# Reordering the first chunk of a fused attention, gated-product and MoE kernel

## The chip, the cores and the metric

The kernel runs on one core of one Trainium2 chip. The metric is the device time of one execution in microseconds (us). The engines are named as in the profile: PE is TensorE, with PEld its weight loads; DVE is VectorE, ACT ScalarE, POOL GpSimd, and SP is SyncE, which issues most of the DMA transfers.

## The reference

Three stages follow one another. First comes attention with a sliding window of 128 positions and a linear bias per head, for 4 batches of 8 heads, 576 positions and 64 columns:

```
rel = pos[:, None] - pos[None, :]
mask = (rel >= 0) & (rel < 128)
scores = where(mask, q @ k.T / 8 + bias, -1e9)
x = softmax(scores) @ v            # then laid out as [2304, 512]
```

Then a gated product, `x = ((x @ w_a) * (x @ w_b)) @ w_out`, with an inner width of 1536. Last, a mixture of eight experts with top-1 choice:

```
logits = x @ w_gate + modality_bias[modality_id]
e = argmax(logits);  gate_w = softmax(logits)[e]
out = gate_w * (relu(x @ w1[e]) @ w2[e])     # e per token, F = 1024
```

The weights of the gated product arrive as 64-bit floats.

## The kernel before

The 2304 tokens are cut into 7 chunks of 3, 2, 2, 3, 3, 3 and 2 tiles of 128 (`CH`). An item is one pair of heads on one tile of one chunk: scores on PE, masking and maximum on DVE, the exponential on ACT, the reciprocal on DVE, the normalisation on ACT, PE transposes (`pt_tr`), copies into `pc` (half ACT, half DVE), masks by POOL into `pt`, and the product with v on PE. Chunk 0 has 12 items (`n0`). They run first, as a software pipeline of attention alone; items `n0` and `n0 + 1`, the first two of chunk 1, are scored in it too.

From then on the gated product of chunk c goes in 12 steps of 128 inner columns (`NJ`): `step0` for chunk 0, `step` for chunks 1 to 5, `step6` for the last. Each step holds, beside its own matmuls, some items of the attention of the next chunk. A step j of PE is: `psa` (12 matmuls into the bank ab0), `psb` (12 into ab1), the attention's matmuls, and `mm_out` of the step before (`pend`). DVE forms `gf = psb * asb`, where ACT copied `asb` from `psa`. psb of the next step may start only when gf has read its bank. Numbers in the 32-bit format of the matmuls are split in a high and a low half, and three of the four products are kept; in chunk 0 `mm_out` multiplies the unsplit 32-bit weight and gf instead (L506).

In chunk 0 the 64-bit weights are also converted: `wab_jobs(j)` gives five jobs for w_a and w_b of step j, `one` and twice `more` on DVE (together `f64_ops`), `hi` on ACT and `rest` on DVE. `wo_jobs(j)` gives three on DVE for w_out. The raw and the converted w_out tiles share four rotating buffers (`WOB`). DVE's row in `step0` mixes these jobs with the items' reciprocals, `rest` first.

A tile of x that leaves the gated product is routed: its eight logits, the largest and its index, the gate, and the rank of each token within its expert. The logits come either from PE (four transposes, L522, and eight matmuls with the gate weights, L530), or, for chunks listed in `RD`, from DVE: eight dots of a 128x512 tile with a broadcast gate weight (`rd_dot`, L592, one expert per step, each tile of the chunk). These dots stand in step j = 1 to 8 of the next chunk. The rest (`route_fin`) is one short row of DVE instructions (stage a, L537 to L556), a gate (L549, L550), and a rank, for which PE multiplies by a triangle (`tri`) and adds `ones` times `osum`; DVE then adds the tile's one-hot to `osum` (L567), so that ranks follow one another.

The order on PE, DVE and ACT is the order in which the program is written from chunk 0's steps on. SP's and POOL's are made by a scheduler.

Of the kernel before, what the change touches and what calls it, by code (L numbers as in the profile page):

```python
# [21 lines left out]
def attn_moe_moe2(ctx: ExitStack, tc, q, k, v, moe_w_a, moe_w_b, moe_w_out, modality_id,  # L22
# [185 lines left out]
    def a_prep_q(a):  # L208
        n = a.nt * P
        if a.c not in S32:  # L210
            for h in range(2):
# [556 lines left out]
    with tc.manual_schedule():  # L768
# [74 lines left out]
        st_s(n0 + 1)
        i1 = live[n0 + 1]
        score_red(i1)
        score_inv(i0)
        score_nrm(i0)
        pt_tr(i0)
        score_exp(i1)
        pt_cp(i0)  # L850
# [621 lines left out]
```

## Time and profile before

| | |
|---|---|
| runs (us) | 829.16, 830.38, 830.48 |
| median (us) | 830.38 |
| profiled execution (us) | 828.85 |
| its span (us) | 827.1 |
| mean granted clock of TensorE | 0.993 |
| busy: PE, DVE, ACT, POOL | 97%, 66%, 56%, 28% |
| DMA | 145 MB, 175 GB/s on average |

Of the 40 equal slices of the span, PE is busy for 90% or more in 37. The others are the second (80%), the third (70%; 41 to 62 us, the change from the pipeline to chunk 0's steps) and the last. A row of a timeline is an instruction or a run of equal ones; its duration includes what overlaps with the next, so the distance of two starts is the better measure of what one costs. The square bracket names what ended the engine's idle time.

### The profile page before, as it was taken

To read this page: it belongs to the slowest core of one execution; us is meant where nothing else is said; L and a number is where in the kernel's file an instruction comes from. 1 tells how busy PE (TensorE), PEld (TensorE's weight loads), DVE (VectorE), ACT (ScalarE), POOL (GpSimd) and SP (SyncE) were. 2 spreads that over 40 slices of the span, in tenths; PEclk is the share of its full clock that TensorE was granted. 3 is DMA by queue.
4 is the path that set the end of the run, shared out by engine and by line. 5 is a ranking of instruction groups with operands and counts; after the bars stand their busy time and mean duration, and the time that the engine had idled before them with its cause. 6 is when DMAs were issued, how large, how long until landed. Compare 5 with 4: busy or idle time off the path is not lost.

```text
span 827.1 us, 14384 instructions
## 1 busy us (share of the span) xinstructions
PE 798.5 (97%) x4686; PEld 722.1 (87%) x4686; DVE 547.4 (66%) x1571; ACT 461.3 (56%) x1161; POOL 235.3 (28%) x365
## 2 busy tenths in 40 slices
PE   9879999999999999999999999999999999999994
PEld 7767877999899999999999999998888998989893
DVE  7789997777676776767876776378476444447420
ACT  6854446877688866666667643223436444547410
POOL 5353231533333333333333332020233030115101
PEclk9999999999999999999999999999999999999998
DMA  8994346677666875555556444467428554549201
GB/s 241 369 381 138 121 130 204 198 222 229 183 163 176 206 191 163 146 159 133 161 159 152 127 128 123 140 225 218 145 90 300 186 186 127 180 128 323 107 16 41
DMA packets 78629, 145.13 MB, mean 175 GB/s; under 512 B 14095, under 2 KB 41903, under 8 KB 78544
## 3 DMA queue, kind: packets, MB, share of 16 engines
q1 hardware_dynamic: 74992, 134.39, 53.5%
q0 software_dynamic: 3552, 9.73, 3.2%
q8 instruction: 39, 0.64, 0.3%
q14 instruction: 46, 0.38, 0.1%
HBM read 118.16 MB, written 22.12 MB: 170 GB/s over the span
## 4 chain that ended last, share of the span: by engine, by line
PE 61%; DVE 13%; issue 9%; ACT 7%; DMA 5%; POOL 2%; SPq 2%; POOLq 0%; ACTq 0%; DVEq 0%
PE ps_ab L493 24%; PE acc L510 10%; PE ps_h L1225 8%; PE ps_y L1208 8%; PE acc L506 3%; PE ps_o L369 2%; PE ps_s L251 2%; DVE f64f L417 1%; ACT p L275 1%; DVE junk L592 1%; DMA wraw<-in_moe_w_a 1%; PE ps_p L303 1%; DVE p L265 1%; ACT g L1063 1%; DMA kk<-in_k 1%
## 5 line engine op out<-in xcount | busy, mean ns | idle before, releaser
L493 PE MATMUL ps_ab<-xr,wab 128*128 128x384 f32 (+1 forms) x2016 | 325.6, 316 | 3.6 <-DVE gf L1126 3.0
L493 PEld LDWEIGHTS ps_ab<-xr,wab 128*128 128x128 f32 x2016 | 307.7, 189 | 14.9 <-issue 4.6
L510 PE MATMUL acc<-wo,g 128*128 128x512 f32 x540 | 136.0, 395 | 0.0
L319 POOL TENSOR_SCALAR_AFFINE_SELECT pt<-pc 128x512 fp32r<-128x512 f32 (+1 forms) x72 | 47.2, 656 | 263.2 <-DVE pc L317 240.6
L510 PEld LDWEIGHTS acc<-wo,g 128*128 128x128 f32 x540 | 97.7, 190 | 17.0
L1225 PE MATMUL ps_h<-xT,w1s 128*128 128x384 f32 x576 | 104.3, 337 | 0.0
L1208 PE MATMUL ps_y<-w2s,h 128*128 128x512 f32 x432 | 104.0, 394 | 0.0
L1225 PEld LDWEIGHTS ps_h<-xT,w1s 128*128 128x128 f32 x576 | 99.7, 188 | 1.3 <-issue 0.5
L1208 PEld LDWEIGHTS ps_y<-w2s,h 128*128 128x128 f32 x432 | 79.7, 188 | 15.7
L275 ACT ACTIVATE p<-p,mx 128x128 f32<-128x128 f32 x144 | 56.7, 395 | 29.8 <-DVE mx L265 29.6
L592 DVE CUSTOM_DVE_ANT_0 junk<-x,wgt 128x512 f32<-128x512 f32 x88 | 62.4, 709 | 2.5 <-DMA wgt<-in_wgt 0.5
L378 ACT COPY u<-ps_o 64x384 f32<-64x384 f32 x120 | 56.9, 474 | 7.8 <-PE ps_o L369 6.4
L294 ACT ACTIVATE p<-p,mx 128x128 f32<-128x128 f32 x120 | 41.8, 395 | 26.7 <-DVE mx L283 26.5
L1063 ACT CAST g<-gf 128x384 fp32r<-128x384 f32 (+1 forms) x60 | 28.2, 471 | 50.6 <-DVE gf L1061 50.1
L1064 DVE TENSOR_TENSOR g<-gf,g 128x384 fp32r<-128x384 f32 (+1 forms) x60 | 30.3, 505 | 37.6 <-ACT g L1063 37.6
L875 DVE TENSOR_TENSOR w2s<-wr,w2s 128x1024 fp32r<-128x1024 f32 x24 | 29.4, 1225 | 38.0 <-ACT w2s L874 37.9
L1215 POOL DMA_INDIRECT out<-y,idx x18 | 21.2, 1176 | 114.9 <-ACT y L1214 113.3
L1061 DVE TENSOR_TENSOR gf<-ps_ab,asb 128x384 f32<-128x384 f32 (+1 forms) x60 | 30.1, 502 | 32.4 <-PE ps_ab L493 25.4
L1228 ACT ACTIVATE h<-ps_h 128x384 fp32r<-128x384 f32 x48 | 23.6, 491 | 44.3 <-PE ps_h L1225 40.8
L321 POOL TENSOR_SCALAR_AFFINE_SELECT pt<-pc 128x512 fp32r<-128x512 f32 (+1 forms) x72 | 48.2, 669 | 0.0
L875 DVE TENSOR_TENSOR w1s<-wr,w1s 128x1024 fp32r<-128x1024 f32 x28 | 34.3, 1224 | 16.6 <-ACT w1s L874 14.2
L1229 DVE SCALAR_TENSOR_TENSOR h<-ps_h,h 128x384 fp32r<-128x384 f32 x48 | 26.3, 554 | 27.8 <-ACT h L1228 27.6
(216 smaller groups left out, 1202.4 us busy)
## 6 DMA issues: line engine op xcount, KB each, us to landing
wo<-wo_d SPq DMA_DIRECT2D x60, 512.0 KB
wr<-in_moe_w SPq DMA_DIRECT2D x56, 512.0 KB
wgt<-in_wgt SPq DMA_DIRECT2D x32, 256.0 KB
wraw<-in_moe_w_a SPq DMA_DIRECT2D x12, 512.0 KB
wraw<-in_moe_w_b SPq DMA_DIRECT2D x12, 512.0 KB
wor<-in_moe_w_out SPq DMA_DIRECT2D x12, 512.0 KB
wo_d<-wo SPq DMA_DIRECT2D x12, 512.0 KB
kr<-in_k SPq DMA_DIRECT2D x24, 256.0 KB
```

What stands on the lines that cost most here:

```text
L275: nc.scalar.activation(out=it.p[:, h, :], in_=it.p[:, h, :], func=AF.Exp, bias=it.mx[:, 2 + h:3 + h], scale=-1.0, accum_out=it.mx[:, 4 + h ...
L294: nc.scalar.activation(out=it.p[:, h, :], in_=it.p[:, h, :], func=AF.Copy, scale=it.mx[:, 6 + h:7 + h])
L319: nc.gpsimd.affine_select(out=it.pt[:, :, 0], in_=pc, pattern=pat + [[-1, P]], base=0, channel_multiplier=1, compare_op=ALU.is_gt, fill=0.0)
L321: mark["pt"] = nc.gpsimd.affine_select(out=it.pt[:, :, 1], in_=pc, pattern=pat + [[1, P]], base=0, channel_multiplier=-1, compare_op=ALU.i ...
L378: nc.scalar.copy(out=u[o:o + 64], in_=it.po[o:o + 64, 1 - h:4 - h])
L493: nc.tensor.matmul(ps[:, :n], lhsT=w[:, m, r, kk * P:(kk + 1) * P], rhs=xr[:, s, kk, :n], start=(idx == 0), stop=(idx == len(terms) - 1))
L510: nc.tensor.matmul(acc[c, t], lhsT=g[:, r, t * P:(t + 1) * P], rhs=w[:, s, :], start=(j == 0 and idx == 0), stop=(j == NJ - 1 and idx == 2))
L592: nc.vector.tensor_tensor_reduce(out=junk, in0=x2[:, 0:DM], in1=wgt[0][:, e % 2], scale=1.0, scalar=0.0, op0=ALU.mult, op1=ALU.add, accum_ ...
L875: nc.vector.tensor_tensor(out=dst[:, 1], in0=srcw, in1=dst[:, 0], op=ALU.subtract)
L1063: nc.scalar.copy(out=gt[:, 0, :n], in_=gf[:, :n])
L1208: nc.tensor.matmul(pss[t], lhsT=h[:, r, f, t * P:(t + 1) * P], rhs=W2[f // 2][:, s_, f % 2, :], start=(f == 0 and i == 0), stop=(f == 7 an ...
L1225: nc.tensor.matmul(ps, lhsT=W1[f // 2][:, r, kk, (f % 2) * P:(f % 2 + 1) * P], rhs=xT[:, s_, kk, :], start=(kk == 0 and i == 0), stop=(kk ...
```

## The change

It has five parts.

A. Items `n0` and `n0 + 1` are no longer scored in the first pipeline. In their place a new `step00` does step 0: it scores both, computes gf(0), converts weights, and starts step 1. The matmuls of a and b of step 0 begin within chunk 0's attention, in pieces by `kk` (0 and 1, then 2, then 3). For this the last three attention outputs use the acc banks instead of ab0 and ab1. One job fewer of weights is converted in the pipeline.

B. In `step0`, `wo_load(j + 1)` and `wo_jobs(j)` stand one step earlier: `mm_out(j - 1)` in step j reads a weight that was converted in step j - 1.

C. `consts_b` (five small POOL operations) moves from step 2 to step 9 (`CJ`), and the tile `tinit` shares the buffer x2T instead of asb.

D. `RD` holds chunk 1 too: its two tiles are routed by dots on DVE in chunk 2.

E. In the last chunk the three tiles of chunk 5 are ranked by a table of steps: stage a of two in step 8 and of the third in step 9, both behind `gf`; ranks 0 and 1 in step 10 ahead of psb, and rank 2 in step 11.

```diff
-    RD = (2, 3, 4, 5)
+    RD = (1, 2, 3, 4, 5)
-    CJ = 2
+    CJ = 9
...
+        it.po = ps_acc.tile([P, 2, 2 * P], F32, tag=f"ab{g % 2}" if g < n0 - 3 else f"acc{g % 3}", name="ps_o")
...
-        if 0 <= g < n0 + 2:
+        if 0 <= g < n0:
...
+            if n0 - 2 <= g:
+                mm_ab(0, 0, g - n0 + 2, (0, 1))
...
+    def step00():
+        n, p1 = CH[0] * P, pairs[1, 0]
+        w1, w2, wo = job.pop(1)[3:], wab_jobs(2), wo_jobs(0)
+        job[2] = w2
+        i0 = live[n0] = score_mm(p1, 0)
+        mm_ab(0, 0, 0, (3,))
+        i1 = live[n0 + 1] = score_mm(p1, 1)
+        mm_ab(0, 0, 1, (3,))
+        w1[0]()
+        score_red(i0)
+        w1[1]()
...
+        score_exp(i0)
+        score_inv(i0)
+        score_red(i1)
+        prep_va(p1)
+        score_nrm(i0)
+        mm_ab(0, 1, 0)
+        wo[0]()
+        pt_tr(i0)
+        pt_cp(i0)
+        prep_vd(p1)
+        score_exp(i1)
+        for f in (w2[0], wo[1], w2[1], wo[2], w2[2], w2[3]):
+            f()
+        new_preps(goal[2], goal[0])
+        return (0, 0, gf), [n0 + 1], [n0]
 def step0(j, pend, sc, tp):
-        dw = [f for i in ((j - 1, j) if last else (j - 1,)) if i >= 0 for f in wo_jobs(i)]
+        dw = wo_jobs(j)
-        psa = mm_ab(0, j, 0, None if j else 1)
+        psa = mm_ab(0, j, 0) if j > 1 else ab_ps[0]
...
 def step6(j, pend):
-        for _ in range(2 if j == NJ - 1 else 1):
-            if ranks and ranks[0][0] == 2:
-                next(ranks.pop(0)[1], None)
-        for r in ranks:
-            if r[0] < 2:
-                next(r[1])
-                r[0] += 1
+        if j < E and ranks:
+            next(ranks.pop(0)[1], None)
+        for _ in range({E + 2: 2, E + 3: 1}.get(j, 0)):
+            next(ranks.pop(0), None)
         psb = mm_ab(c, j, 1)
...
+        if j == E:
+            ranks[:] = [r[1] for r in ranks]
+        for i in {E: (0, 1), E + 1: (2, 0, 1), E + 2: (0,)}.get(j, ()):
+            next(ranks[i])
...
-                if j:
-                    wo_load(j)
+                if j + 1 < NJ:
+                    wo_load(j + 1)
...
+                pend, sc, tp = step0(j, pend, sc, tp) if j else step00()
```

Lines of the changed kernel are some 9 to 36 higher than before. First, PE at the change from the pipeline to the steps, before (`ps_ab_650` and `ps_ab_729` are a and b of step 0, `ps_ab_776` and `ps_ab_791` those of step 1, `ps_p` the transposes of an item's p, `ps_o` its product with v):

```order
L346 MATMUL ps_ot<-ident,u 128x128
L247 MATMUL ps_s<-kk,qq 128x256 x2
L493 MATMUL ps_ab_650<-xr_131,wab_469 128x384 x3
L493 MATMUL ps_ab_729<-xr_131,wab_469 128x384 x12
L303 MATMUL ps_p<-ident,p 128x128 x4
L493 MATMUL ps_ab_776<-xr_131,wab_633 128x384 x12
L493 MATMUL ps_ab_791<-xr_131,wab_633 128x384 x12
L369 MATMUL ps_o<-pt,vv 128x2x128 x8
L247 MATMUL ps_s<-kk,qq 128x256 x2
L506 MATMUL acc_845<-f64o,gf 128x512
```

And now, from the last pieces of step 0 on (`ps_ab_727` and `ps_ab_789` are a and b of step 1):

```order
L254 MATMUL ps_s<-kk,qq 128x256 x2
L502 MATMUL ps_ab_585<-xr_131,wab_469 128x384 x3
L254 MATMUL ps_s<-kk,qq 128x256 x2
L502 MATMUL ps_ab_617<-xr_131,wab_469 128x384 x3
L502 MATMUL ps_ab_727<-xr_131,wab_702 128x384 x12
L310 MATMUL ps_p<-ident,p 128x128 x2
L502 MATMUL ps_ab_789<-xr_131,wab_702 128x384 x12
L378 MATMUL ps_o<-pt,vv 128x2x128 x4
L310 MATMUL ps_p<-ident,p 128x128 x2
L254 MATMUL ps_s<-kk,qq 128x256 x2
L515 MATMUL acc_840<-f64o,gf 128x512
```

The transposes of both items stood ahead of step 1's a; now those of the first stand between its a and its b, and those of the second behind both and behind the first one's product with v, with the third item's scores and mm_out (acc) after them.

DVE in the same place, before, from gf of step 1 to the reciprocal that the next item waits for (`wab` is a `rest`, `mx` with TENSOR_SCALAR the item's maximum):

```order
L443 TENSOR_TENSOR wab_834<-f64f,wab_834 128x2x512
L281 TENSOR_SCALAR mx<-mx 128x2
L413 TENSOR_SCALAR f64f<-wraw_694 128x1024
L413 TENSOR_SCALAR f64o<-wor 128x512
L417 SCALAR_TENSOR_TENSOR f64f<-wraw_694,f64f 128x1024
L283 RECIPROCAL mx<-mx 128x2
L417 SCALAR_TENSOR_TENSOR f64f<-wraw_694,f64f 128x1024
```

And now, the last rows of step 0 and the first of step 1, up to the reciprocal of the second item:

```order
L422 TENSOR_SCALAR f64f<-wraw_206 128x1024
L426 SCALAR_TENSOR_TENSOR f64o<-wor,f64o 128x512
L426 SCALAR_TENSOR_TENSOR f64f<-wraw_206,f64f 128x1024
L426 SCALAR_TENSOR_TENSOR f64o<-wor,f64o 128x512
L426 SCALAR_TENSOR_TENSOR f64f<-wraw_206,f64f 128x1024
L452 TENSOR_TENSOR wab_761<-f64f,wab_761 128x2x512
L288 TENSOR_SCALAR mx<-mx 128x2
L422 TENSOR_SCALAR f64f<-wraw_209 128x1024
L422 TENSOR_SCALAR f64o<-wor 128x512
L426 SCALAR_TENSOR_TENSOR f64f<-wraw_209,f64f 128x1024
L290 RECIPROCAL mx<-mx 128x2
```

The second item's maximum and reciprocal stand behind the whole conversion of step 2's weight (`wraw_206`), its `rest` (`wab_761`), and half of step 3's; before, both items were through ahead of step 1's `rest`.

DVE in one step of chunk 2, before (a step with a tile's routing from PE's logits):

```order
L177 TENSOR_TENSOR kk<-kr_2_2233,kk 128x2x512
L537 TENSOR_TENSOR lg<-ps_l,bm 128x8
L539 MAX m_2940<-lg 128x8
L541 MAX_INDEX ix<-m_2940,lg 128x8
L543 TENSOR_SCALAR sc<-m_2940 128x1
L555 CAST sc<-ix 128x1
L556 TENSOR_SCALAR oh<-iot,sc 128x8
L1061 TENSOR_TENSOR gf<-ps_ab_2954,asb 128x256
L1064 TENSOR_TENSOR g<-gf,g 128x256
L317 TENSOR_TENSOR pc<-ps_p,pc 128x256
```

And now, one such step (`junk` are the dots):

```order
L288 TENSOR_SCALAR mx<-mx 128x2
L290 RECIPROCAL mx<-mx 128x2
L177 TENSOR_TENSOR kk<-kr_2_2233,kk 128x2x512
L601 ISA junk,lgr<-x_2779,wgt 128x512
L601 ISA lgr 128x1
L601 ISA junk,lgr<-x_2782,wgt 128x512
L601 ISA lgr 128x1
L1096 TENSOR_TENSOR gf<-ps_ab_2944,asb 128x256
L1099 TENSOR_TENSOR g<-gf,g 128x256
L324 TENSOR_TENSOR pc<-ps_p,pc 128x256
L266 COPY_PREDICATED ps_s<-upper,ps_s 128x2x128
```

The short row of routing from `ps_l` is gone there, and two dots of 512 columns stand ahead of `gf` in this step and seven others.

Last, PE in steps 10 and 11 of the last chunk, before (`ps_ab_7785` and `ps_ab_7810` are a and b of step 10):

```order
L493 MATMUL ps_ab_7785<-xr_7136,wab_1416 128x256 x12
L565 LDWEIGHTS tri
L565 MATMUL ps_r<-oh,tri 128x8
L566 LDWEIGHTS ones
L566 MATMUL ps_r<-osum,ones 128x8
L493 MATMUL ps_ab_7810<-xr_7136,wab_1416 128x256 x12
L510 MATMUL acc_7316<-wo,g 128x512 x3
L510 MATMUL acc_7317<-wo,g 128x512 x3
L493 MATMUL ps_ab_7836<-xr_7136,wab_1487 128x256 x12
```

And now (`ps_ab_7800` and `ps_ab_7835` are a and b of step 10):

```order
L502 MATMUL ps_ab_7800<-xr_7154,wab_1415 128x256 x12
L574 LDWEIGHTS tri
L574 MATMUL ps_r<-oh,tri 128x8
L575 LDWEIGHTS ones
L575 MATMUL ps_r<-osum,ones 128x8
L574 LDWEIGHTS tri
L574 MATMUL ps_r<-oh,tri 128x8
L575 LDWEIGHTS ones
L575 MATMUL ps_r<-osum,ones 128x8
L502 MATMUL ps_ab_7835<-xr_7154,wab_1415 128x256 x12
L519 MATMUL acc_7334<-wo,g 128x512 x3
```

In step 10 two ranks instead of one stand between a and b. On DVE, the rows between the last dot of chunk 5 and the first `osum` are now gf of step 8, stage a of two tiles, gf of step 9, stage a of the third, two gates and the low half of an expert's weight (w1s); before, stage a of all three came first.

## Rows read from the trace of the kernel before

**Rows 1.** The page's part 1: busy us, share, instructions of each engine.
```profile
PE 798.5 (97%) x4686; PEld 722.1 (87%) x4686; DVE 547.4 (66%) x1571; ACT 461.3 (56%) x1161; POOL 235.3 (28%) x365
```

**Rows 2.** Waits of PE: engine, line, releaser: us in total, times, longest.
```profile
PE acc L506 <- DVE f64o L417: 4.7, 5, 2.0
```

**Rows 3.** PE's timeline, start of chunk 0: start, us, operation, [idle before].
```profile
30.12 1.10 PE L247 MATMUL ps_s<-kk,qq 128*128 128x256 f32 x4 [0.63 <-POOL qq L220]
...
33.37 0.41 PE L303 MATMUL ps_p<-ident,p 128*128 128x128 f32 x2 [0.97 <-ACT xr L352]
...
43.74 0.62 PE L303 MATMUL ps_p<-ident,p 128*128 128x128 f32 x2 [1.46 <-ACT p L294]
44.12 4.41 PE L493 MATMUL ps_ab<-xr,wab 128*128 128x384 f32 x24
...
50.39 1.03 PE L247 MATMUL ps_s<-kk,qq 128*128 128x256 f32 x4
53.40 2.84 PE L506 MATMUL acc<-f64o,gf 128*128 128x512 f32 x6 [1.98 <-DVE f64o L417]
55.68 4.72 PE L493 MATMUL ps_ab<-xr,wab 128*128 128x384 f32 x24
```

**Rows 4.** DVE's timeline, the same stretch.
```profile
44.56 0.55 DVE L992 TENSOR_TENSOR gf<-ps_ab,asb 128x384 f32<-128x384 f32 x1
45.03 1.21 DVE L417 SCALAR_TENSOR_TENSOR f64f<-wraw,f64f 128x1024 uint32<-128x1024 uint32 x1
47.18 0.42 DVE L317 TENSOR_TENSOR pc<-ps_p,pc 128x256 fp32r<-128x256 f32 x1 [0.94 <-ACT pc L316]
48.13 1.26 DVE L443 TENSOR_TENSOR wab<-f64f,wab 128x1024 fp32r<-128x1024 f32 x1 [0.53 <-ACT wab L440]
...
59.31 0.16 DVE L283 RECIPROCAL mx<-mx 128x2 f32<-128x2 f32 x1
```

**Rows 5.** Windows: length, then busy us of PE, PEld, DVE, ACT, POOL; clock.
```profile
80.00:88.00 8.00, 8.00 (x38) 6.37 (x37) 7.73 (x17) 5.17 (x13) 0.08 (x2) 1.00 0.36 112
212.30:267.40 55.10, 54.66 (x411) 51.38 (x410) 36.77 (x140) 42.71 (x125) 20.70 (x38) 1.00 0.59 162
580.00:584.00 4.00, 4.00 (x18) 3.51 (x18) 1.99 (x10) 1.71 (x4) 0.00 (x0) 0.57 0.56 197
```

**Rows 6.** PE's timeline, chunk 2, steps 9 and 10.
```profile
258.79 2.98 PE L493 MATMUL ps_ab<-xr,wab 128*128 128x256 f32 x24
...
264.14 2.98 PE L493 MATMUL ps_ab<-xr,wab 128*128 128x256 f32 x24
```

**Rows 7.** DVE in chunk 2: all of L281, then one of its rows.
```profile
L281 DVE TENSOR_SCALAR mx<-mx x10: 158/169/171, 214.3 to 265.3; 128x2 f32<-128x2 f32 x10
...
260.34 0.17 DVE L281 TENSOR_SCALAR mx<-mx 128x2 f32<-128x2 f32 x1 [0.73 <-ACT p L275]
```

**Rows 8.** DVE's timeline, chunk 4.
```profile
373.77 0.17 DVE L281 TENSOR_SCALAR mx<-mx 128x2 f32<-128x2 f32 x1 [0.74 <-ACT p L275]
...
380.49 0.17 DVE L281 TENSOR_SCALAR mx<-mx 128x2 f32<-128x2 f32 x1 [0.73 <-ACT p L275]
...
382.03 0.68 DVE L592 CUSTOM_DVE_ANT_0 junk<-x,wgt 128x512 f32<-128x512 f32 x1
...
384.10 0.55 DVE L1061 TENSOR_TENSOR gf<-ps_ab,asb 128x384 f32<-128x384 f32 x1
...
387.74 0.17 DVE L281 TENSOR_SCALAR mx<-mx 128x2 f32<-128x2 f32 x1 [0.74 <-ACT p L275]
```

**Rows 9.** Steps 8 and 9 of the last chunk: PE, then DVE.
```profile
579.70 2.29 PE L493 MATMUL ps_ab<-xr,wab 128*128 128x256 f32 x12 [2.77 <-DVE gf L1126]
...
576.24 0.16 DVE L537 TENSOR_TENSOR lg<-lgr,bm 128x8 f32<-128x8 f32 x1
...
579.23 0.42 DVE L1126 TENSOR_TENSOR gf<-ps_ab,asb 128x256 f32<-128x256 f32 x1
```

**Rows 10.** L592 between 290 and 296 us: durations in ns, min/median/max.
```profile
L592 DVE CUSTOM_DVE_ANT_0 junk<-x,wgt x2: 825/890/954, 292.3 to 293.3; 128x512 f32<-128x512 f32 x2
```

More of the change, by code (lines that the diff above doesn't have):

```diff
@@ L215, in a_prep_q, with qq_new, q_scale @@
         if a.c > 0:
-            a.qq = at.tile([P, 2, MT * P], F32, tag="qq", bufs=2, name="qq")
+            qq_new(a)
+        q_scale(a)
+    def qq_new(a):
+        a.qq = at.tile([P, 2, MT * P], F32, tag="qq", bufs=2, name="qq")
         for h in range(2):
-            o, d = 64 * h, 64 * (1 - h)
-            if a.c > 0:
-                nc.gpsimd.memset(a.qq[d:d + 64, h, :n], 0.0)
+            nc.gpsimd.memset(a.qq[64 - 64 * h:128 - 64 * h, h, :a.nt * P], 0.0)
+    def q_scale(a, hs=(0, 1)):
+        n = a.nt * P
+        for h in hs:
+            o = 64 * h
             if a.c == 0 and a.hp < QD and h == 1:
@@ L482, in wo_split, with mm_ab @@
         nc.sync.dma_start(out=wo_d[j], in_=w.bitcast(F32))
-    def mm_ab(c, j, m, part=None):
+    def mm_ab(c, j, m, kks=tuple(range(KD))):
         n = CH[c] * P
         xr, w = xr_t[c], wab[j]
-        if part is None or part == 0:
+        if 0 in kks:
             ab_ps[m] = ps_acc.tile([P, MT * P], F32, tag=f"ab{m}", name=f"ps_ab{m}")
@@ L491, in mm_ab @@
         for idx, (kk, r, s) in enumerate(terms):
-            if part is None or part == (kk == KD - 1):
+            if kk in kks:
                 nc.tensor.matmul(ps[:, :n], lhsT=w[:, m, r, kk * P:(kk + 1) * P], rhs=xr[:, s, kk, :n],
@@ L724, in consts_ap @@
     def consts_ap():
-        cl[1] = tinit = m1.tile([P, TI * TW], I32, tag="asb", bufs=1, name="tinit")
+        cl[1] = tinit = m1.tile([P, TI * TW], I32, tag="x2T", bufs=1, name="tinit")
         nc.gpsimd.iota(tinit, pattern=[[0, TI * TW]], base=N, channel_multiplier=1)
@@ L791, in attn_moe_moe2 @@
         job[1] = wab_jobs(1)
-        conv += wab_jobs(0) + job[1][:4]
+        conv += wab_jobs(0) + job[1][:3]
         def st(lim, f, g, *x):
@@ L805, in conv_step @@
                 conv.pop(0)()
-        ns = n0 + 2
         for g in range(-SK, n0):
@@ L811, in attn_moe_moe2 @@
             st(n0, pv_tr, g - 2)
-            if g + SK <= n0:
-                st_s(g + SK)
+            st_s(g + SK)
+            if n0 - 2 <= g:
+                mm_ab(0, 0, g - n0 + 2, (0, 1))
             r = g + SK - 1
-            if r <= n0:
-                st(ns, score_sel, r)
+            st(n0, score_sel, r)
             st(n0, pv_x, g - 3, 1)
-            if r <= n0:
-                st(ns, score_max, r)
-            st(ns, score_inv, g)
+            st(n0, score_max, r)
+            st(n0, score_inv, g)
             st(n0, pt_cp, g)
-            st(ns, score_exp, g + 1)
+            st(n0, score_exp, g + 1)
             conv_step(g)
@@ L825, in attn_moe_moe2 @@
             st(n0, pv_x, g - 2, 0)
-            if g >= -1 and (g + PRP) % CH[0] == 0 and g < n0 - CH[0]:
+            if g >= -1 and (g + PRP) % CH[0] == 0 and g < n0 - CH[0] - 1:
                 a_preps(g + PRP + CH[0])
+            if g == n0 - 4:
+                qq_new(pairs[1, 0])
             if g == CAP - SK:
@@ L831, in attn_moe_moe2 @@
                 consts_ad()
-        l1, l2, i0 = (live[n0 + k] for k in (-1, -2, 0))
+        l1, l2, p1 = live[n0 - 1], live[n0 - 2], pairs[1, 0]
         pv_x(live[n0 - 3], 1)
@@ L835, in attn_moe_moe2 @@
         pv_tr(l2)
-        pv_ev(l1)
-        mm_ab(0, 0, 0, 0)
+        mm_ab(0, 0, 0, (2,))
+        mm_ab(0, 0, 1, (2,))
+        q_scale(p1, (0,))
         pv_x(l2, 0)
         pv_x(l2, 1)
+        q_scale(p1, (1,))
+        pv_ev(l1)
         pv_tr(l1)
@@ L842, in attn_moe_moe2 @@
         pv_x(l1, 1)
[L843 to L850, printed above, removed]
+        pos["prep"] += 1
     assert not conv
@@ L964, in attn_moe_moe2 @@
     pend = None
+    def step00():
[9 more added lines that the diff above has]
+        w1[1]()
+        asb = m1.tile([P, MT * P], F32, tag="asb", bufs=1, name="asb")
+        nc.scalar.copy(out=asb[:, :n], in_=ab_ps[0][:, :n])
+        gf = m1.tile([P, MT * P], F32, tag="g", bufs=2, name="gf")
+        nc.vector.tensor_tensor(out=gf[:, :n], in0=ab_ps[1][:, :n], in1=asb[:, :n], op=ALU.mult)
+        score_exp(i0)
[12 more added lines that the diff above has]
+        new_preps(goal[2], goal[0])
+        cur["s"] = goal[0]
+        return (0, 0, gf), [n0 + 1], [n0]
     def step0(j, pend, sc, tp):
@@ L969, in step0 @@
         new = list(range(cur["s"], goal[j]))
-        its = [live[g] for g in tp] if j else []
+        its = [live[g] for g in tp]
         if j + 2 < NJ:
@@ L975, in step0 @@
         da = [job.pop(j + 1)[4]] if j + 1 in job else []
-        da += js[:3 if j else 2]
+        da += js[:3]
         di = [f for g in sc for f in score_invs(live[g])]
-        dw = [f for i in ((j - 1, j) if last else (j - 1,)) if i >= 0 for f in wo_jobs(i)]
+        dw = wo_jobs(j)
         db = di[:1] + dw[:1] + di[1:] + dw[1:]
@@ L992, in step0 @@
         nc.vector.tensor_tensor(out=gf[:, :n], in0=psb[:, :n], in1=asb[:, :n], op=ALU.mult)
-        for f in () if j else js[2:3]:
-            f()
         for it in its:
@@ L1012, in step0 @@
         new_preps(goal[j + 2], goal[j])
-        if pend is not None:
-            mm_out(*pend, wo_t[j - 1])
+        mm_out(*pend, wo_t[j - 1])
         if last:
@@ L1019, in step0 @@
         cur["s"] = goal[j]
-        for g in tp if j else ():
+        for g in tp:
             live.pop(g)
-        return (0, j, gf), new, sc if j else tp + sc
+        return (0, j, gf), new, sc
     def step(c, j, pend, sc, tp):
```

4 lines of the change are left out of this document (1 added, 3 removed).

## The prediction

> **What bounds the kernel now.** The page's first part is read first: TensorE (PE) is busy for 97% of the span and VectorE (DVE) for 66% [rows 1]. A change pays, then, where it takes away PE's idle time or PE's instructions, and it costs where it makes PE wait for an engine that has no room. The list of PE's waits comes next; its largest entry is mm_out waiting for the converted output weight: 4.7 us in five waits, the longest 2.0 [rows 2]. Last come the timelines of the three places where the change puts something else: the first steps of chunk 0, chunk 2, and steps 8 to 10 of the last chunk. In chunk 0 the reader is to see that DVE has no spare time (7.73 of 8.00 us) although its share of the whole span is 66%; in chunk 2 it has 36.77 us of work in 55.10 us, while PE has 54.66 [rows 5]. The average of DVE thus says nothing of either place.
>
> **Times.** The profiled execution took 828.85 us for a span of 827.1. The median of the runs is 830.38, 1.5 us more. I sum against 828.85 and add 1.5 at the end.
>
> **Start of chunk 0 (chunk 1's first two items moved; a and b begun within the attention; weights a step ahead).** Before psa(1) at 44.12, PE waited 0.63 us for the item's q, 0.97 for an xr copy that stood behind the items' work, and 1.46 for the item's p, and spent 0.38 on that item's transposes [rows 3]. All four now lie behind, so psa(1) starts near 44.12 - 3.4 = 40.7, and gf(0), which read its bank at 44.56 [rows 4], near 41. That is the gain, and it isn't kept. On PE, pt_tr of the second item (i1) now stands behind psa(1) and psb(1), and mm_out(0) behind it. Its p waits for the reciprocal of i1, which DVE does as the last but a few in its new row. Before, gf(0) to that reciprocal took 44.56 to 59.31, 14.75 us, with 0.94 and 0.53 of waiting in it [rows 4]. In the new row between the same two instructions one f64f (1.21 less its overlap, 1.14), one rest of a weight (1.18) and gf(1) (0.47) are gone, and a maximum with its reciprocal (0.32) and the low half of v (0.47) are new: 14.75 - 1.47 - 2.79 + 0.79 = 11.3 us of work. From 41 that gives 52.3 without a wait, 53.8 with as much waiting as before; I take 53.1. Then ScalarE's first normalisation (0.7 us with its hand-over) brings PE to pt_tr at 53.8, though PE was free for it by about 47.5 (psb(1) ends at 40.7 + 4.25, and four products with a wait for GpSimd follow). The wait is near 6 us. Transposes (0.25) and scores (1.03) lead to mm_out(0) at 55.1, and its six matmuls to psa(2) at 57.4 (2.28 later, as from 53.40 to 55.68). Before, psa(2) started at 55.68 [rows 3]: +1.7 us there.
>
> After that the weight that mm_out reads is a step old, so the other four waits of that list go: 4.7 - 2.0 = 2.7 us [rows 2]. Whether PE can use them depends on DVE, which works 7.73 of 8 us in such a step [rows 5] and starts 1.7 us late. f64o(j) now waits for mm_out(j-2), since the four rotating buffers hold raw and converted weights; queued behind it on DVE are the next weight's operations, but that mm_out is long issued, so I give it nothing. The moved loads stand one step earlier on SP's queue, among transfers that run until 60 us; a late third load would hold DVE about 1 us there, inside the range.
>
> [...]
>
> So chunk 0 ends at +1.7 - 2.7 = -1.0 with no clock loss, and at +0.7 with all of it, with DVE as the brake on either. I take +0.2, range -2.5 (the reciprocal comes without waits and DVE keeps up) to +2.5 (nothing of the 2.7 is won back). consts_b on GpSimd moves from step 2 to step 9; GpSimd is idle in most of a step, so nothing; at worst the 5 us delay one selection by that much once, which the range holds.
>
> **Chunk 2 (chunk 1's two tiles routed by dots).** The tiles' transposes and logits leave PE, and 16 dots of 128x512 go on DVE, two in each of steps 1 to 8, between the k, q or v conversion and gf. What decides is DVE's turn from one item's maximum (L281) to the next, in which each instruction waits for the one before or for ScalarE's answer to it. In chunk 4, which has three dots per step, a turn is 6.72 us with a v half in it (373.77 to 380.49) and 7.25 with a k half (to 387.74), and the three dots take 382.03 to 384.10, 2.07 us [rows 8]. There PE's own step is longer than that, so nothing is seen. Two dots are 1.36; dropping the third takes 0.71, and 256 instead of 384 columns in gf, its copy and its low half about 0.37 (an estimate: L1061's 0.55 us at 384.10 against the 0.42 of L1126 at 579.23 [rows 9], thrice). A turn is then 5.64 (v), 6.17 (k), and with a q half 4.97 (260.34 to 265.3 [rows 7]) + 1.36 = 6.33. PE's own step without routing is 264.14 - 258.79 = 5.35 [rows 6]. Every turn with dots is longer than PE's step, so PE waits for DVE. Three v, three k and two q turns make 48.1, and step 9 has 4.97 and two groups of about 1.0 (like the three from 576.24 to 579.23 [rows 9]): 55.1. Before, the nine turns took 51.0 [rows 7]. DVE had some 0.95 us in hand at the end: the last maximum was at 265.3, its p ready near 266.5 (a reciprocal and ScalarE's answer), and PE came for it 3.3 us into its step that began at 264.14, at 267.4. So **+4.1 - 0.95, about +3.0**. Bounds: the dots fit into DVE's idle third, -2.8 (below); dots are slowed by GpSimd and step 9 pays in full, +5.
>
> On the upper bound: a dot beside GpSimd's additions took 0.95 and 0.82 us (from 292.3) where one without them takes 0.68 [rows 8, 10]. [...]
>
> **Last chunk (ranks dealt out).** psb(9) waited 2.77 us for gf(8), which stood behind three routing groups from 576.24 to 579.23 [rows 9]. gf(8) now stands ahead, so this wait goes, with its clock loss: 2.8 + 1.7. But step 10 now has two ranks in front of psb(10), and the second's matmul with ones needs DVE's osum of the first. By DVE's new row that comes after gf(8) and its low half (to 577.5), two groups (579.5), gf(9) and its half (580.4), the third group (581.4), two gates (0.7) and a 1.2 us conversion of an expert's weight that waits for ScalarE: near 584. psa(10) ends near 581, so PE waits about 3 us again, at half clock afterwards. I take -0.3; from -4.5 (that conversion is early) to +1.
>
> **Sum.** +0.2 + 3.0 - 0.3 = +2.9 on 828.85: 831.75, and with 1.5 a median of **833.3 us**.
>
> **Rivals.**
> - *The dots hide (the other side).* DVE is idle for a third of chunk 2 [rows 5], and 16 dots of 0.69 are 11 us in 18 us of idle time. If the waits inside a turn shrink with it, so that a turn stays at or below 5.35 us, PE gains: nine steps at 5.35 are 48.15 against 264.14 - 212.3 = 51.8, of which 0.8 is left for ranks, so -2.8. Then -2.8 + 0.2 - 0.3: 827.5. Against it: those waits are answers of ScalarE to DVE's own instruction, and don't move. It decides at a turn of 5.35 us.
> - *The start costs more.* The full bubble, half clock after it and DVE behind for the rest of chunk 0: +2.5, and with chunk 2 at +3.8, 836.5.
> - *The parts cancel.* The late waits of chunk 0 are won back (-2) and the last chunk's stall is gone for good (-2 or more) while chunk 2 costs 3 to 4: about 830.5.
>
> **Chances.** Slower as forecast, or more: 0.52, of which 0.15 for the second rival. The third rival: 0.26. The first: 0.22, with those cases in which both stalls go and chunk 2 costs little. Differences within 0.2% (1.7 us) can't be told from none here. The range: low end 826.5, the first rival with 1 us of the start's gain; high end 837.5, the second rival with chunk 2 near its bound. Beside it, the forecast's own range is 832 to 836.
>
> **What would show it.** Right: PE waits 4 to 6 us for ScalarE's p (now L301) in 45 to 55 us and mm_out no longer for f64o; turns of DVE in chunk 2 of 5.6 to 6.4 us with PE waiting in each; a PE wait on osum (L576) of 2 to 3 us before psb(10) and none on gf(8). Wrong: psa(2) before 55 us, chunk 2 no longer than its 70 us, or no wait before psb(10).

## The result and the profile after

The changed kernel took a median of 835.18 us (834.57 to 837.31, four runs) against 829.93 for the kernel before (829.16 to 830.48, four runs). The ratio is 1.0069, 95% interval 1.0048 to 1.0089: slower, by 5.3 us. The forecast was 833.3, slower, with a range of 826.5 to 837.5. The profiled execution of before (828.85) is quicker than its four timed runs, that of after (837.31, span 835.5) as slow as the slowest of its own, so the traces differ by more (8.4 us) than the medians.

Where PE stands at some marks in the two traces:

| mark | before | after | difference |
|---|---|---|---|
| psa of step 2, chunk 0 | 55.7 | 59.0 | +3.3 |
| chunk 1, step 0 | 139.3 | 141.2 | +1.9 |
| chunk 2, step 1 | 212.4 | 213.9 | +1.6 |
| chunk 2, step 10 | 264.1 | 267.6 | +3.5 |
| chunk 3, step 1 | 282.2 | 288.2 | +6.1 |
| last chunk, psa of step 9 | 575.4 | 583.6 | +8.2 |
| last chunk, last mm_out | 592.0 | 600.5 | +8.5 |
| end of the span | 827.1 | 835.5 | +8.4 |

Chunk 2 is the largest part: 69.8 us from its step 1 to chunk 3's step 1 before, 74.3 after.

The waits of PE in the changed kernel (us in total, times, longest) are the first thing to read beside [rows 2]:

```profile
PE ps_p L310 <- ACT p L301: 10.5, 10, 7.3
PE ps_r L575 <- DVE osum L576: 3.3, 2, 2.9
PE ps_ab L502 <- DVE gf L1158: 2.2, 2, 2.0
```

Waits for f64o are gone. The first line has grown from 2.1 us and holds both large terms of the forecast: one wait of 7.3 us at the start and seven of chunk 2, 2.8 us together. The second line is the new wait of the last chunk. The third is another thing, below.

PE at the start of chunk 0 after, for [rows 3]. Of the fifteen matmuls in the first row three end step 0; the other twelve are psa(1), from 40.07 on, and the row at 42.49 is psb(1):

```profile
39.35 3.16 PE L502 MATMUL ps_ab<-xr,wab 128*128 128x384 f32 x15
42.35 0.38 PE L310 MATMUL ps_p<-ident,p 128*128 128x128 f32 x2
42.49 2.33 PE L502 MATMUL ps_ab<-xr,wab 128*128 128x384 f32 x12
45.27 0.38 PE L378 MATMUL ps_o<-pt,vv 128*128 128x256 f32 x1 [0.46 <-POOL pt L326]
46.32 0.62 PE L378 MATMUL ps_o<-pt,vv 128*128 128x256 f32 x3 [0.66 <-POOL pt L328]
54.24 0.77 PE L310 MATMUL ps_p<-ident,p 128*128 128x128 f32 x2 [7.30 <-ACT p L301]
54.80 1.91 PE L254 MATMUL ps_s<-kk,qq 128*128 128x256 f32 x4
56.51 3.03 PE L515 MATMUL acc<-f64o,gf 128*128 128x512 f32 x6
58.97 4.73 PE L502 MATMUL ps_ab<-xr,wab 128*128 128x384 f32 x24
```

PE is through with the first item's product at 46.9 and then waits for the second item's p. The four score matmuls behind the wait take 1.91 us where they took 1.03. What DVE does in the meantime, for [rows 4]:

```profile
40.38 0.55 DVE L986 TENSOR_TENSOR gf<-ps_ab,asb 128x384 f32<-128x384 f32 x1
...
50.19 1.23 DVE L452 TENSOR_TENSOR wab<-f64f,wab 128x1024 fp32r<-128x1024 f32 x1 [1.11 <-ACT wab L449]
...
53.53 0.16 DVE L290 RECIPROCAL mx<-mx 128x2 f32<-128x2 f32 x1
```

From gf(0) to the reciprocal 13.2 us pass, behind a whole weight's conversion.

The turns of DVE in chunk 2 after, for [rows 7] and [rows 8]; the rows are the maximum of an item, the dots between two of them, and what was converted:

```profile
239.95 0.17 DVE L288 TENSOR_SCALAR mx<-mx 128x2 f32<-128x2 f32 x1 [0.74 <-ACT p L282]
...
240.23 1.33 DVE L177 TENSOR_TENSOR kk<-kr,kk 128x1024 fp32r<-128x1024 f32 x1
241.48 0.68 DVE L601 CUSTOM_DVE_ANT_0 junk<-x,wgt 128x512 f32<-128x512 f32 x1
...
242.21 0.69 DVE L601 CUSTOM_DVE_ANT_0 junk<-x,wgt 128x512 f32<-128x512 f32 x1
...
246.10 0.17 DVE L288 TENSOR_SCALAR mx<-mx 128x2 f32<-128x2 f32 x1 [0.74 <-ACT p L282]
...
252.42 0.17 DVE L288 TENSOR_SCALAR mx<-mx 128x2 f32<-128x2 f32 x1 [0.74 <-ACT p L282]
...
258.04 0.17 DVE L288 TENSOR_SCALAR mx<-mx 128x2 f32<-128x2 f32 x1 [0.74 <-ACT p L282]
```

A turn is 6.15 us with k in it, 6.32 with q, 5.62 with v (the first v and k turns of the stretch took 5.48 and 6.05). The forecast had 6.17, 6.33 and 5.64. DVE waits 0.73 or 0.74 us for ACT in each turn, whatever is put into it.

The last chunk after, for [rows 9], psa of step 10, the ranks and psb:

```profile
588.45 1.68 PE L502 MATMUL ps_ab<-xr,wab 128*128 128x256 f32 x12
...
593.10 0.17 PE L575 MATMUL ps_r<-osum,ones 128*128 128x8 bf16 x1 [2.90 <-DVE osum L576]
593.12 2.91 PE L502 MATMUL ps_ab<-xr,wab 128*128 128x256 f32 x12
```

gf(8) is no longer waited for, and the second rank is: 2.90 us in place of 2.77, and 2.91 us for the twelve matmuls behind it, at a granted clock of 0.58 in 593 to 597 us.

The third of the waits listed above lies ahead of psb(5) of the last chunk, where nothing was changed: a dot of DVE waited for its gate weight to arrive.

```profile
564.21 0.69 DVE L601 CUSTOM_DVE_ANT_0 junk<-x,wgt 128x512 f32<-128x512 f32 x1 [2.93 <-DMA wgt<-in_wgt]
```

The same load made DVE wait 0.45 us in the trace of before, 2.93 here; PE lost 2.0 us by it. In the traces of the kernels below that load makes DVE wait 2.2 and 2.0 us in two and 0 to 1.2 in the others, with the code there unchanged, so I put it down to the execution and not to the change; it accounts for nearly all of the 2.1 us that the table's difference grows from chunk 3 to psa(9).

### The profile page after: what moved, and what is told of

Same layout as the page of the kernel before. It is cut to its first block, busy times and chain, and to the rows that moved or that the text cites. A ratio compares the mean times of both kernels' runs of the same rounds, so it can differ in the third digit from the quotient of the medians.

```text
span 835.5 us, 14380 instructions
## 1 busy us (share of the span) xinstructions
PE 801.8 (96%) x4662; PEld 720.9 (86%) x4662; DVE 558.9 (67%) x1603; ACT 460.6 (55%) x1159; POOL 234.6 (28%) x365
## 3 DMA queue, kind: packets, MB, share of 16 engines
q1 hardware_dynamic: 76144, 136.48, 54.2%
## 4 chain that ended last, share of the span: by engine, by line
PE 64%; DVE 14%; issue 9%; ACT 9%; DMA 2%; POOL 1%; POOLq 0%; SPq 0%; ACTq 0%; DVEq 0%
PE ps_ab L502 25%; PE acc L519 9%; PE ps_h L1261 9%; PE ps_y L1244 8%; PE acc L515 3%; ACT p L282 2%; PE ps_o L378 2%; PE ps_s L258 2%; DVE junk L601 2%; PE ps_p L310 2%; PE ps_s L254 1%; DMA wgt<-in_wgt 1%; DVE f64f L426 1%; DVE g L1099 1%; ACT g L1098 1%
## 5 line engine op out<-in xcount | busy, mean ns | idle before, releaser
L326 POOL TENSOR_SCALAR_AFFINE_SELECT pt<-pc 128x512 fp32r<-128x512 f32 (+1 forms) x72 | 46.5, 646 | 261.8 <-DVE pc L324 236.3
L601 DVE CUSTOM_DVE_ANT_0 junk<-x,wgt 128x512 f32<-128x512 f32 x104 | 73.4, 706 | 5.3 <-DMA wgt<-in_wgt 2.9
L328 POOL TENSOR_SCALAR_AFFINE_SELECT pt<-pc 128x512 fp32r<-128x512 f32 (+1 forms) x72 | 46.6, 647 | 0.0
```

What stands on the lines that cost most here:

```text
L326: nc.gpsimd.affine_select(out=it.pt[:, :, 0], in_=pc, pattern=pat + [[-1, P]], base=0, channel_multiplier=1, compare_op=ALU.is_gt, fill=0.0)
L328: mark["pt"] = nc.gpsimd.affine_select(out=it.pt[:, :, 1], in_=pc, pattern=pat + [[1, P]], base=0, channel_multiplier=-1, compare_op=ALU.i ...
L601: nc.vector.tensor_tensor_reduce(out=junk, in0=x2[:, 0:DM], in1=wgt[0][:, e % 2], scale=1.0, scalar=0.0, op0=ALU.mult, op1=ALU.add, accum_ ...
```

## The experiments

The theory to be tested: DVE's serial turn in chunk 2 (part D) is nearly all of the loss; the start (A and B) and the last chunk (E) each trade one wait for another. Rivals: the loss is the start's, or the stall at the end, or DVE's mere amount of work. Ratios are to the kernel before on the same chip; 0.1% is 0.8 us.

**Chunk 1 routed on PE again.**

```diff
-    RD = (1, 2, 3, 4, 5)
+    RD = (2, 3, 4, 5)
```

> The changed kernel with part D alone undone: chunk 1's two tiles are again routed from PE's logits. Theory (DVE's serial turn in chunk 2 costs 4.5 us from chunk 2's step 1 to chunk 3's step 1): 4 to 5 us under the changed kernel's 835.2, so 830.2 to 831.2, with that stretch back at about 69.8 us (74.3 in the changed kernel). Rival (the loss is the start's and the last chunk's, the dots move only idle time): 834 or more, since what chunk 2 lost would have been lost elsewhere.

Measured: 832.10 us, ratio 1.0021 (1.0011 to 1.0032). The stretch is back at 70.0 us. By the ratios 0.48%, 4.0 us, are D's, the low end of what was expected. The rival falls.

**One rank in step 10, two in step 11.**

```diff
-        for _ in range({E + 2: 2, E + 3: 1}.get(j, 0)):
+        for _ in range({E + 2: 1, E + 3: 2}.get(j, 0)):
...
-        for i in {E: (0, 1), E + 1: (2, 0, 1), E + 2: (0,)}.get(j, ()):
+        for i in {E: (0, 1), E + 1: (2, 0, 1), E + 2: (1,)}.get(j, ()):
```

> The changed kernel, but in the last chunk one rank stands ahead of psb in step 10 and two in step 11 (the changed kernel has two and one). Theory (PE's 2.9 us wait for osum and the half clock after it, 1.5 us, are part E's price): 4.4 us less, 830.8. Rival (the expert's weight or the table of ranks ends later anyway, so the wait moves to the first expert matmul): 834 to 835.

Measured: 832.61 us, ratio 1.0021 (1.0007 to 1.0034), again 4.0 us by the ratios, where 4.4 were expected; the rival falls. The longest wait for osum is 0.8 us, and psa(9) to psb(11) takes 11.5 us instead of 15.4 (15.1 before). So E as written gains nothing, though E could: its stall was only moved.

**The second item's reciprocal early.**

```diff
-        for f in (w2[0], wo[1], w2[1], wo[2], w2[2], w2[3]):
+        w2[0]()
+        score_inv(i1)
+        score_nrm(i1)
+        for f in (wo[1], w2[1], wo[2], w2[2], w2[3]):
             f()
```

> The changed kernel, but the reciprocal and the normalisation of item n0+1 stand in step00 behind the first conversion of step 2's weight instead of behind step 2's whole conversion. Theory (PE's 7.3 us wait is DVE's order, and DVE has some room behind it): PE's wait under 1.5 us, step 2's a at 51 to 52 us instead of 59.0, chunk 1 at 136 to 139 us instead of 141.2, so 2 to 5 us less: 830 to 833. Rival (DVE is full in chunk 0, and the wait only shows it): PE's wait goes but comes back as waits for gf or converted weights, chunk 1 at 140.5 or later, 834.5 or more.

Measured: 836.16 us, ratio 1.0064 (1.0045 to 1.0082): nothing, and chunk 1 starts at 141.8. My theory's numbers failed here and the rival's held. PE in that kernel, then ACT:

```profile
46.23 0.38 PE L310 MATMUL ps_p<-ident,p 128*128 128x128 f32 x2
50.68 2.07 PE L254 MATMUL ps_s<-kk,qq 128*128 128x256 f32 x4 [4.07 <-ACT qq L232]
52.55 4.87 PE L515 MATMUL acc<-f64o,gf 128*128 128x512 f32 x6
56.85 4.73 PE L502 MATMUL ps_ab<-xr,wab 128*128 128x384 f32 x24
...
63.68 0.62 PE L310 MATMUL ps_p<-ident,p 128*128 128x128 f32 x2 [1.63 <-ACT p L301]
...
67.18 4.72 PE L502 MATMUL ps_ab<-xr,wab 128*128 128x384 f32 x24
```

```profile
49.17 1.04 ACT L449 CAST wab<-f64f 128x1024 fp32r<-128x1024 f32 x1 [3.03 <-DVE f64f L426]
50.12 1.03 ACT L232 ACTIVATE qq<-qr,qscale 64x256 f32<-64x256 f32 x2
```

The 7.3 us wait is gone, but a few rows on PE waits 4.1 us for the next item's q, which stands on ACT behind a weight's cast that waits for the same DVE conversions. psa(2) is 2.1 us earlier, and psa(3) stands at 67.18 against 67.27: no gain. DVE is busy 22.5 of the 26 us from 41 to 67 in both (23.1 before), which fits the rival: its conversions set the pace.

**The dots in DVE's gaps.** In chunk 2 one dot goes between gf and its low half and one between an item's maximum and its reciprocal.

```diff
+        gap = c == 2 and now and DJ <= j < DJ + E
-        if now and DJ <= j < DJ + E:
+        if now and DJ <= j < DJ + E and not gap:
             rd_dot(j - DJ)
...
         nc.scalar.copy(out=gt[:, 0, :n], in_=gf[:, :n])
+        if gap:
+            rd_dot(j - DJ, (0,))
...
         for g in new:
             score_exp(live[g])
+        if gap:
+            rd_dot(j - DJ, (1,))
```

> The changed kernel, but in chunk 2 the two dots of a step stand where DVE waits for ACT anyway: one between gf and its low half (a gap of 0.47 us), one between an item's maximum and its reciprocal (0.74 us). The same work in another place. Theory (it is the serial turn that counts): a turn grows by about 0.25 instead of 1.36 us, to 4.5 to 5.3 us, under PE's 5.35; chunk 2's stretch from its step 1 to chunk 3's step 1 67 to 69.5 us, and 5 to 7 us less in all: 828 to 830. Rival (DVE's amount of work, or the dots' use of memory beside POOL): the stretch stays above 73 us and the time above 833.5.

Measured: 833.18 us, ratio 1.0033 (1.0019 to 1.0047); the stretch 71.7 us. The same dots in another place cost 2.6 us less in the trace (3.0 by the ratios), so the place counts. But that is half of what the theory said: turns were 5.4 to 5.9 us, not under 5.35, and the stretch isn't under 70. One turn, DVE:

```profile
249.95 0.41 DVE L288 TENSOR_SCALAR mx<-mx 128x2 f32<-128x2 f32 x1
...
252.12 0.68 DVE L601 CUSTOM_DVE_ANT_0 junk<-x,wgt 128x512 f32<-128x512 f32 x1
...
254.59 1.05 DVE L601 CUSTOM_DVE_ANT_0 junk<-x,wgt 128x512 f32<-128x512 f32 x1
255.58 0.42 DVE L288 TENSOR_SCALAR mx<-mx 128x2 f32<-128x2 f32 x1
```

and some steps earlier the dot in the second gap, with POOL beside it:

```profile
237.59 1.05 DVE L601 CUSTOM_DVE_ANT_0 junk<-x,wgt 128x512 f32<-128x512 f32 x1
237.47 0.63 POOL L328 TENSOR_SCALAR_AFFINE_SELECT pt<-pc 128x512 fp32r<-128x512 f32 x1
238.08 0.89 POOL L393 TENSOR_TENSOR xf<-xf,z 128x128 f32<-128x128 f32 x1
238.93 0.45 POOL L392 TENSOR_TENSOR xf<-u 128x128 f32<-128x128 f32 x1
```

The dot in the first gap takes 0.68 us. The one in the second begins 0.12 us behind POOL's mask and takes 1.05; the mask takes its usual 0.63, and POOL's addition, which begins behind the dot, 0.89 instead of 0.46. Of two that overlap here the later one is the longer. The second gap is where POOL masks, so it hid less than its length. That the two hinder each other is read from these times; by what means was not shown.

**A and B, two by two,** with chunk 1 routed on PE and ranks at one and two. The base has neither (C and E alone); B is `wo_load(j + 1)` and `wo_jobs(j)`; A is step00 and the pieces of a and b, with `wo_jobs(j - 1)`.

```diff
-        dw = wo_jobs(j)
+        dw = [f for i in ((j - 1, j) if last else (j - 1,)) for f in wo_jobs(i)]
```

> The kernel before with parts C and E alone, E with one rank in step 10 and two in step 11; chunk 1 routed on PE. Base of a two by two of parts A (the start) and B (w_out a step ahead). Theory: psb(9) of the last chunk no longer waits for gf (2.8 us) and PE's clock stays up (1.7), psa(9) to psb(11) 11.5 us instead of 15.1: 3.6 us under the kernel before, about 827.0. Rival (the first expert's weight or the ranks end that stretch anyway): 829.5 to 830.7.

> The base with part B alone: w_out's weight loaded and converted a step ahead, items n0 and n0+1 still scored in the first pipeline. Theory (A makes the start's loss, B takes away PE's waits for f64o, as far as DVE lets it): PE waits for f64o 4.7 us in the base, none here; chunk 1 starts 0 to 2.5 us earlier than before's 139.3, time 0 to 2.5 us under the base. Rival (B's conversion ahead of step 2's weight is itself the loss, since DVE is full there): chunk 1 at 140.5 or later, 1 us or more above the base.

> The base with part A alone: step00 and the pieces of a and b within the attention, but w_out's weight converted in the step that needs it. Theory (DVE decides the start: the second item's reciprocal and step 3's weight come late since the items' work lies among the conversions): PE still waits 4 us or more for that item's p, and mm_out waits for f64o as before; chunk 1 at 140.5 to 142, 1 to 2.5 us above the base. Rival (A is free once B's conversions are out of its way): chunk 1 at 139.3 or earlier, no more than the base.

> The base with A and B: the changed kernel with chunk 1 routed on PE and ranks at one and two. Theory (the parts add; A+B moves chunk 1's start to 141.2 to 142.8, as in four traces so far): 1.9 to 3 us above the base, about 829 to 830. Rival (B pays for A once the stalls at the end are gone): the base's time or less.

| | ratio (interval) | median | chunk 1 in the trace | PE's waits in 40 to 150 us |
|---|---|---|---|---|
| base | 0.9980 (0.9960 to 1.0000) | 827.50 | 141.8 | f64o 4.9, p 1.5 |
| B | 0.9990 (0.9975 to 1.0005) | 829.42 | 141.9 | p 5.2 |
| A | 0.9975 (0.9960 to 0.9991) | 828.37 | 142.5 | p 5.6, f64o 2.6 |
| A and B | 0.9982 (0.9969 to 0.9996) | 828.33 | 142.7 | p 8.0 |

The base's stretch from psa(9) to psb(11) takes 11.1 us in its trace, 4 us less than before, as the theory had it; its ratio gives a gain of 1.7 us (0 to 3.3), about half of the 3.6 expected, though the medians are 2.5 us apart. The four can't be told apart by their ratios, each of which is known to 0.15 to 0.2%: a price of the start of up to about 2 us could hide there. Part B takes away all of PE's waits for f64o (4.9 us), and 3.7 us come back as waits for p; part A halves them, and 4.1 us come back. In time, the losses that the theories expected of A and of the two together are not there, so the start costs nothing measurable; but chunk 1 is at 140.5 or later in all four traces, as the rival on B had it, and not at 139.3 or earlier, as the rival on A had it. The base, whose order there is that of before, has it at 141.8, and the base with the spread dots below, with that order too, at 140.9: the trace of before was a lucky one. The nine matmuls of step 0's a show part of why; they took 1.81 us at 36.67 there, and in the base:

```profile
36.56 2.95 PE L493 MATMUL ps_ab<-xr,wab 128*128 128x384 f32 x9
```

with a granted clock of 0.62 in 36 to 40 us, where before had 1.00. So the table's +1.9 at chunk 1 compares two levels of the clock as much as two kernels. The runs say the same: of the base's twelve, seven had a mean clock of 0.991 or more and took 826.2 to 827.6 us, and five 0.984 to 0.988 and took 829.7 to 831.7; the 36 runs with A, B or both had 0.986 to 0.991 and took 827.4 to 831.2. In the traces the clock in 40 to 52 us was 1.00 in the base and 0.74 (B), 0.83 (A) and 0.82 (both) in the other three, within or behind PE waits of 3.3, 5.6 and 7.3 us; in 52 to 64 us it was 0.86 in the base and 0.97, 0.75 and 0.75 in the others.

**D alone on the same base,** A, C and E with the change's own dots:

> Parts A, C, E (ranks at one and two) and the change's own part D: two dots in each of steps 1 to 8, both between conversion and gf. Theory: 4 us above the same kernel routed on PE (ratio 0.9975), so ratio 1.002 to 1.003; turns of 5.6 to 6.4 us. Rival (D's loss needs the late start that B brought, or the last chunk's stall): ratio under 1.0.

Measured: 832.18 us, ratio 1.0032 (1.0021 to 1.0043) against 0.9975: 4.7 us by the ratios (3.8 by the medians) are D's, with no late start by B and no stall at the end. The rival falls.

**The dots spread over ten steps.** One dot per step between gf and its low half, a second only in steps with v or k; the two groups, gates and ranks follow behind them, in step 11 and in chunk 3.

```diff
...
+        if now and c == 2 and j == DJ:
+            dq.extend((e, t) for e in range(E) for t in (0, 1))
+        if dq and j % 3 != 0:
+            dot1()
...
         nc.scalar.copy(out=gt[:, 0, :n], in_=gf[:, :n])
+        if dq:
+            dot1()
```

> The kernel with parts A, C and E (ranks at one and two), and chunk 1 routed by dots, but spread over steps 1 to 10: one dot per step between gf and its low half, where DVE waits 0.47 us for ACT (it cost 0.68 us there when two dots stood in DVE's gaps; the one beside POOL's masks cost 1.05), and a second one only in steps whose conversion is of v or k. Theory (a dot costs what it adds to DVE's serial turn beyond PE's 5.35 us): turns of 5.2 (v), 5.7 (k) and 5.2 us (q), on average PE's step; chunk 2's step 1 to chunk 3's step 1 67 to 69 us (70.0 with routing on PE, 74.3 in the change), and 1 to 3 us less than the same kernel routed on PE (ratio 0.9975): ratio 0.994 to 0.996. Rival (the dots delay ACT, POOL or the ranks behind them): ratio 0.9975 or more.

> The same spread dots on the base without A (parts C and E alone, ratio 0.998). Theory: 1 to 3 us less than the base, ratio 0.9945 to 0.997. Rival: no less than the base.

Measured: 827.48 us, ratio 0.9967 (0.9956 to 0.9978), with A; 826.20, ratio 0.9971 (0.9955 to 0.9986), without. Both are faster than the two kernels of this case, by 0.3% against before. DVE's turns with A:

```profile
231.95 0.17 DVE L288 TENSOR_SCALAR mx<-mx 128x2 f32<-128x2 f32 x1 [0.74 <-ACT p L282]
...
237.17 0.17 DVE L288 TENSOR_SCALAR mx<-mx 128x2 f32<-128x2 f32 x1 [0.74 <-ACT p L282]
...
242.99 0.17 DVE L288 TENSOR_SCALAR mx<-mx 128x2 f32<-128x2 f32 x1 [0.74 <-ACT p L282]
...
248.00 0.17 DVE L288 TENSOR_SCALAR mx<-mx 128x2 f32<-128x2 f32 x1 [0.74 <-ACT p L282]
```

They are 5.22 (v), 5.82 (k) and 5.01 (q; 4.97 without a dot [rows 7]), PE's steps 5.42, and PE waits only 0.2 us in steps 1 to 9: 48.8 us against 51.9 with routing on PE. From step 10 to chunk 3's step 1, however, it takes 20.2 us against 18.0, since the groups, gates and ranks now stand there. The stretch is 69.1 and 68.7 us, where 67 to 69 were expected and the change has 74.3: the same 16 dots, so the rival that DVE's mere amount of work makes the loss falls here. The gain of 0.1% over each base is less than I had expected and within the intervals.

## Why the prediction was right, point by point

- **Chunk 2.** Right in mechanism, and in the turns to 0.02 us but for the first two, which were 0.1 to 0.2 us shorter. The slowing by GpSimd that made the upper bound did not come: all 16 dots took 0.68 or 0.69 us. The forecast had step 9 to 10 as 6.97 us; it took 7.05. PE came to step 10's transposes 4.73 us later than before, 3.2 of them lost since step 1: the forecast's +3.0. What was mis-sized is the price of the whole part, 4.5 us in the trace and 4.0 and 4.7 by ratios. The other 1.3 us are lost behind step 10's transposes, for which I had put no term. DVE's rows there:

```profile
272.24 0.14 DVE L558 TENSOR_SCALAR sc<-sc 128x1 f32<-128x1 f32 x1
...
278.00 0.15 DVE L576 TENSOR_TENSOR osum<-osum,oh 128x8 bf16<-128x8 bf16 x1
...
281.31 0.81 DVE L413 TENSOR_TENSOR xr<-xf,xr 128x384 fp32r<-128x384 f32 x1 [0.58 <-ACT xr L412]
...
285.80 0.16 DVE L576 TENSOR_TENSOR osum<-osum,oh 128x8 bf16<-128x8 bf16 x1
```

  The two gates (0.6 us from 272.24) and the first rank (0.7 us from 278.00) stand ahead of the copies of x that chunk 3 starts with (281.31); the second rank (285.80) stands behind them, ahead of gf. That these rows are the cause is read from the order; it was not tried.
- **The start.** The size was +0.2 us, and the two by two shows 0.02% between neither and both; with the intervals as they are, the agreement is partly luck. The steps: psa(1) at 40.1 (forecast 40.7), gf(0) at 40.4 (41), the reciprocal at 53.5 (53.1), PE at the transposes at 54.2 (53.8), a wait of 7.3 us (about 6), psa(2) at 59.0 (57.4), since I left a lower clock out of that stretch: 0.74 granted in 54 to 60 us. So psa(2) was 3.3 us later than before, not 1.7. After it the waits for f64o are gone, as forecast, but of the 2.7 us only 1.4 are won by chunk 1. Wrong was to take before's trace for all of its runs: the low clock that I priced as the change's risk is in another execution of the old order too, at another place (0.62 in 36 to 40 us in the base). The 1.7 us of clock loss between -1.0 and +0.7, which is also in the 2.8 + 1.7 of the last chunk, was an estimate from 4.00 us at 0.57 in 580 to 584 us [rows 5]; no run shows this term at the start. The runs show in its place 0.74 in 54 to 60 us behind the wait of 7.3 us, which is 1.6 us by the same sum; and in the last chunk 0.58 in 593 to 597 us behind 2.90 us, but 1.00 behind 2.89 us in the kernel with dots in gaps.
- **The last chunk.** The stall was moved, not removed: +0.3 us in the trace for -0.3 forecast. The row of DVE came as written down, 2.90 us of waiting for osum and a clock of 0.58 after it. The kernel with one rank in step 10 shows that most of the gain I named as the lower bound (-4.5) is there in the trace: 11.5 us for a stretch of 15.1 before.
- **C and the loads.** C shows no wait in the trace; it was not tried alone. The late load for which I had allowed 1 us did not show. But one term that I put at nothing is there: f64o(2) takes the buffer of f64o(0), and I had counted only the matmuls that read it, not the transfer that stores it:

```profile
61.44 0.43 DVE L422 TENSOR_SCALAR f64o<-wor 128x512 uint32<-128x512 uint32 x1 [1.33 <-DMA wo_f<-f64o]
```

  The kernel before has no such wait; the kernel with the second item's reciprocal early, which has part B too, has it once, 1.4 us. What it costs in time was not separated.
- **The rivals.** That the dots hide would have needed turns of 5.35 us, and it was decided there, as said: they were 5.5 to 6.3. That the start costs more was right for the bubble; in time the two by two doesn't show it. That the parts cancel fell with the last chunk, whose stall was not gone.
- **The sum.** 0.2 + 3.0 - 0.3 = 2.9 forecast; 5.3 measured by medians, of which D is 4.0 to 4.7. The start and the last chunk together make up the rest, and that rest, about 1 us, is within the intervals. The sum was right for its largest term, D, which is nearly all of the loss, and 1 to 2 us too small for it.

## What to carry to other kernels

Whether an engine with a third of its time idle could take more work was decided here by the serial turn: add the new instructions to the chain in which it waits for answers to its own work, and compare that turn with the other engine's step (5.48 to 6.32 us against 5.35); idle time that was an answer's delay did not shrink when work was put elsewhere (0.73 or 0.74 us in each of these turns), but work put into such a gap was nearly free (a dot of 0.68 us between gf and its low half added 0.04 to a turn), where no other engine slowed it (beside POOL's mask it took 1.05). Before moving work, look what the wait hides: at the start and at the end of this kernel a wait taken away came back at the next instruction that needed the same engine (of 4.9 us of waits for f64o that part B took away, 3.7 as waits for p; for 2.77 us on gf(8), 2.90 on osum). And take the time of a stage in the old kernel from several executions before pricing a bubble by it.

## What the runs showed of the hardware

TensorE's granted clock fell after a wait or not, with the same rows in that place. In the kernel with dots in gaps a wait of 2.89 us before psb(10) left it at 1.00 in 588 to 592 us:

```profile
588.42 0.17 PE L575 MATMUL ps_r<-osum,ones 128*128 128x8 bf16 x1 [2.89 <-DVE osum L576]
588.44 1.66 PE L502 MATMUL ps_ab<-xr,wab 128*128 128x256 f32 x12
```

In the change 2.90 us in the same place were followed by a clock of 0.58 in 593 to 597 us, and the twelve matmuls took 2.91 us; in the first and the third kernel of the experiments they took 2.03 and 2.52 behind waits of 2.89 and 2.91. In 36 to 40 us the clock was 1.00 in the kernel before and 0.62 in the base, which has the same order there. The length of the wait alone did not decide it in these kernels. Of 35 runs of the kernel before on one chip, those with a mean granted clock of 0.993 or more took 827.6 to 829.5 us, those with 0.987 or less 831.1 to 834.6.

Where a dot of DVE overlapped a mask or an addition of POOL in two stretches, the one that began later took longer than it does alone. In the kernel with dots in gaps, at 237.59, they were the dot, 1.05 us beside the mask, and then the addition, 0.89 instead of 0.46. In the trace of before a dot at 475.36 took 0.68 us, the mask that began behind it at 475.51 took 1.02 instead of 0.63, and the next dot, which began at 476.08 beside that mask, 1.00.
